# Attention and feed-forward on one core: the first chunks' products are rearranged, the interleaving of first and second products starts one chunk earlier, and loads of q, k, v are tied to attention steps

## The chip, the cores and the metric

The kernel runs on one core of one Trainium2 chip. The metric is the device time of a whole execution in microseconds; smaller is better. One run differs from the next by a few tenths of a per cent. Every run has a state, fast or slow; ratios use fast runs alone. A ratio is the mean time of one kernel's fast runs over the mean of the other's fast runs of the same rounds, so it is not quite the ratio of the medians that are quoted beside it. The span that a profile covers is some 1.8 us shorter than the time.

Engines: PE does the matrix products, DVE and ACT the elementwise work, POOL issues the loads (with the cast from 32-bit to bf16), SP issues stores, small copies and DMA transposes.

## The reference, cut to what matters

```python
# q, k, v: (8 batches, 8 heads, 1024 tokens, 64); E, F: (64, 1024)
k_proj = einsum('ks,bhsd->bhkd', E, k)
v_proj = einsum('ks,bhsd->bhkd', F, v)
attn = softmax(q @ k_proj.T / 8)          # over the 64 projected keys
x = attn @ v_proj                         # -> (8192 tokens, 512)
h = maximum(x @ w_in, 0.0)                # 512 -> 2048
out = (h * h) @ w_out                     # 2048 -> 512
```

## The kernel before: the parts that matter

A batch is cut into two chunks of 512 tokens. Chunk (b, c) needs a first product (x times w_in) and a second one (h squared times w_out). Both exist in two forms: a plain one of 64 matmuls of 512 columns, and a seven-product (Strassen-like) one of 112 matmuls of 256 columns. The second form costs PE less but needs sums of blocks, made on DVE. In most of the kernel, here called the woven part, PE alternates between the first product of one chunk and the second product of the chunk before, in numbered steps of 8 matmuls. A chunk takes 28 steps, and a batch, here called a round, takes 56. Attention of the next batches is slipped in at fixed steps. PE's order is written by hand; the other engines are ordered when the program is built.

The attention code:

```python
soft_pool = ctx.enter_context(tc.tile_pool(name="soft", bufs=3))      # 3 buffers of tag "rs"
# ...
def sums_spread(self, pr):              # sums of the exponentials for two pairs of heads
    ps = att_psum()
    # ... 8 matmuls with ones (32 columns each) ...
    inv = soft_pool.tile([P, 2, TCH], F32, tag="rs", name="inv")
    nc.scalar.activation(inv[:], ps[:], AF.Ln)
    nc.scalar.activation(inv[:], inv[:], AF.Exp, scale=-1.0)
    for j in range(2):
        rs = soft_pool.tile([P, 2, TCH], F32, tag="rs", name="rs")
        for a in range(2):
            have = 32 * (2 * a + j)
            for to in (64 * a, 64 * a + 32):
                nc.sync.dma_start(rs[to:to + 32], inv[have:have + 32])   # 8 small copies on SP
        self.rs[pr + j] = rs

def values(self, pr, spare=False):
    e, rs = self.e.pop(pr), self.rs.pop(pr)
    ps = att_psum()                     # the one attention PSUM buffer of the woven part
    # ... 4 matmuls into ps, then DVE: xT = ps * rs
```

One call takes three buffers of the tag "rs": one inv and two rs. There are three such buffers. In the woven part `att_psum()` has a single buffer: what uses it next must wait until ACT or DVE has read it.

The plan of a round in the woven part (t is the round's first step):

```python
for b in range(1, B - 1):
    t = 56 * (b - 1)
    if b > 1:
        on(t + 1, b + 1, "scores", 3)
    on(t + 3, b + 1, "sums_spread", 2)        # second group of sums of batch b+1
    on(t + 7, b + 1, "values", 0)
    on(t + 10, b + 1, "values", 1)
    on(t + 20, b + 1, "values", 2)
    on(t + 23, b + 1, "values", 3)
    # ...
    if b + 2 < B:
        on(t + 2, b + 2, "transpose_q_dma")   # q of batch b+2, DMA transpose on SP
        if b + 3 < B:
            at(t + 2, begin, b + 3)
            on(t + 3, b + 3, "load_q")
        on(t + 30, b + 2, "project")
        on(t + 32, b + 2, "transpose_k_dma")  # DMA transpose of the projected k, on SP
        if b + 3 < B:
            on(t + 34, b + 3, "load_kv")      # 2 x 1 MB (bf16)
        on(t + 44, b + 2, "scores", 0)
        on(t + 47, b + 2, "scores", 1)
        on(t + 50, b + 2, "sums_spread", 0)   # first group of sums of batch b+2
        on(t + 53, b + 2, "scores", 2)
```

The softmax here doesn't subtract the row's maximum and nothing guards it: scores larger than these inputs give would overflow.

Of the kernel before, what the change touches and what calls it, by code (L numbers as in the profile page):

```python
# [9 lines left out]
P = 128  # L10
F32 = mybir.dt.float32
BF16 = mybir.dt.bfloat16
# [7 lines left out]
def kernel(  # L20
# [11 lines left out]
    nc = tc.nc  # L32
# [31 lines left out]
    part_pool = ctx.enter_context(tc.tile_pool(name="part", bufs=5))  # L64
    out_pool = ctx.enter_context(tc.tile_pool(name="outp", bufs=3))
    psum = ctx.enter_context(tc.tile_pool(name="ps", bufs=1, space=bass.MemoryType.PSUM))
    turn = {"att": 0, "bank": 0, "pairs": 2}

    lent = ctx.enter_context(ExitStack())
    pair_pools = [psum, lent.enter_context(tc.tile_pool(name="ps_lent", bufs=1, space=bass.MemoryType.PSUM))]  # L70
# [7 lines left out]

    def bank(shape=(P, 512), dtype=F32, n=None):
        if n is None:  # L80
            turn["bank"] += 1
            n = turn["bank"]
        return psum.tile(list(shape), dtype, tag=f"bank{n % 4}", name="ps_bank")

# [3 lines left out]
    def load(t, src):  # L88
        return nc.gpsimd.dma_start(t, src)

    def load_batch(name, src, b):
        t = qkv_pool.tile([P, H, NI, D], BF16, name=name)
        load(t[:], tokens(src, b))
        return t


# [30 lines left out]
    for j, (lo, hi) in enumerate(W_IN_PIECES):  # L127
        t = wpool.tile([P, NCB, (hi - lo) * P], BF16, name=f"w_in_{lo}")
        load(t[:], w_in_view[:, :, lo * P:hi * P])
        for fb in range(lo, hi):  # L130
            w_in_at[fb] = (t, fb - lo)
        if j < 2:
            load(V0[:, V_PIECES[j + 1]], tokens(v, 0, h=V_PIECES[j + 1]))
    fn = NFB // WP
    for j in range(WP):
        if j == WP - 1:
            load(Q0[:, :, 4:8, :], tokens(q, 0, i=slice(4, 8)))
        t = wpool.tile([P, fn, DM], BF16, name=f"w_out_{j}")
        load(t[:], w_out_view[:, j * fn:(j + 1) * fn, :])
        w_out_sb.append(t)  # L140
# [31 lines left out]
                    *(w_out_sum[:, n, f] for n in range(4)),  # L172
                )

    def sum_w_in(behind):
        with tc.issue_after(behind.queued.ins):
            for lo, hi in W_IN_PIECES[:3]:
                up, (t, j) = w_in_at[lo][0], w_in_at[HF + lo]
                down = t[:, :, j * P:(j + hi - lo) * P]
                n = NCB // 2  # L180
                left_sums(
                    up[:, 0:n], up[:, n:NCB], down[:, 0:n], down[:, n:NCB],
                    *(w_in_sum[:, m, :, lo:hi].rearrange("p c f k -> p c (f k)") for m in range(4)),
                )
# [37 lines left out]
    class Attention:  # L222
# [10 lines left out]
            self.qT = qt_pool.tile([P, H, NT, P], BF16, name="qT")  # L233
            self.e, self.rs, self.ps_x = {}, {}, {}

        def load_kv(self):
            self.K, self.V = load_batch("K_sb", k, self.b), load_batch("V_sb", v, self.b)

        def load_q(self):
            self.Q = load_batch("Q_sb", q, self.b)  # L240


        def keep_k(self, ps_k, g, second=None):
# [53 lines left out]
            )  # L297


        def transpose_q_chunk(self, c, src, hg):  # L300
            ps = bank([P, 4, 2, P], BF16)
            for hh in range(4):
                for n in range(2):
                    nc.tensor.transpose(
                        ps[:, hh, n, :],
                        src[:, 4 * hg + hh, 4 * c + 2 * n:4 * c + 2 * n + 2, :].rearrange("p i d -> p (i d)"), ident[:]
                    )
            nc.vector.tensor_copy(self.qT[:, 4 * hg:4 * hg + 4, 2 * c:2 * c + 2, :], ps[:])

        def transpose_q(self, pr):  # L310
            ps = bank([P, 2, NT, P], BF16)
# [28 lines left out]

        def exponentials(self, ps):
            e = soft_pool.tile([P, 2, TCH], BF16, name="expT", tag="expT", bufs=4)
            nc.scalar.activation(e[:], ps[:], AF.Exp, scale=SCALE)  # L343
            return e

        def inverse(self, ps):
# [49 lines left out]
        def values(self, pr, spare=False):  # L396

            e, rs = self.e.pop(pr), self.rs.pop(pr)
            if spare:
                ps_x = [bank(), bank()]  # L400
            else:
                ps = att_psum()
                ps_x = [ps[:, par] for par in range(2)]
            for o, par, a, r in VALUE_QUADS:
                nc.tensor.matmul(  # L405
                    ps_x[par][o], lhsT=self.vp[r, 2 * pr + a, :], rhs=e[r, par], start=True, stop=True
                )
            for par in range(2):
                nc.vector.tensor_tensor(  # L409
                    out=self.xT[:, pr, :, par], in0=ps_x[par].rearrange("p (c t) -> p c t", c=2),  # L410
                    in1=rs[:, par].rearrange("p (c t) -> p c t", c=2), op=ALU.mult,
                )
# [25 lines left out]
    class Chunk:  # L438
# [5 lines left out]

        def h_tile(self, kh, part):
            if (kh, part) not in self.h:
                self.h[kh, part] = form_pool.tile([P, 2, HF // 2, HC], BF16, name="h", tag="h", bufs=7)
            return self.h[kh, part]

        def sum_x(self):  # L450
            self.x_sum = x_pool.tile([P, 4, NCB // 2, HC], BF16, name="x_sum")
            n = NCB // 2
            x = [self.xT[:, m:m + n, self.c, a] for m in (0, n) for a in range(2)]
            right_sums(*x, *(self.x_sum[:, m] for m in range(4)))
# [253 lines left out]
    with tc.manual_schedule(engines={PE}):  # L708
# [57 lines left out]
        at(2, att.project_v, V_PIECES[2])  # L766
        at(3, att.chunk_values, 0, 1, (1,))
        at(3, nxt.load_kv)
        at(18, sum_w_in, chunk[0, 0])
        at(21, att.transpose_q_chunk, 1, Q0, 0)  # L770
        at(21, att.transpose_q_chunk, 1, Q0, 1)
        at(21, nxt.load_q)
        at(23, att.chunk_scores, 1, 0)
        at(23, att.chunk_scores, 1, 1)
        at(25, att.sums, 0)
        at(27, att.chunk_values, 1, 0)
        at(27, att.chunk_values, 1, 1)
        at(28, sum_w_out, att)
        at(28, begin, 2)
        at(36, nxt.project)  # L780
        at(36, lambda: atts[2].load_kv())
        at(39, nxt.transpose_q, 0)
        at(39, nxt.transpose_q, 1)
        at(39, nxt.transpose_k)
        at(41, nxt.scores, 0)
        at(41, nxt.scores, 1)
        at(44, nxt.transpose_q, 2)
        at(44, nxt.transpose_q, 3)
        at(44, lambda: atts[2].load_q())
        at(45, nxt.sums, 0)  # L790
        at(47, nxt.scores, 2)
        at(49, nxt.scores, 3)
        at(50, nxt.values, 0)
        at(52, nxt.values, 1)
        at(53, nxt.sums, 2)
        at(59, nxt.values, 2)
        at(60, nxt.values, 3)
        at(60, chunk[1, 1].sum_x)
        at(61, lambda: atts[2].project())
        at(59, begin, 3)  # L800
        at(60, lambda: atts[3].load_kv())
        at(61, lambda: atts[2].transpose_q_dma())
        at(61, lambda: atts[3].load_q())
        run_all(chunk[0, 0].first_cold(), chunk[0, 0].second_cold(), chunk[0, 1].first_plain(), chunk[0, 1].second_seven(*(bank()[:] for _ in range(3))))

        nxt = atts[2]
        at(1, nxt.transpose_k)
        at(3, nxt.scores, 0)
        at(5, nxt.scores, 1)
        at(7, nxt.sums_spread, 0)  # L810
        at(9, nxt.scores, 2)
        at(11, nxt.scores, 3)
        turn["pairs"] = 1
        run_all(chunk[1, 0].first_plain())
        lent.close()
        second_pool = ctx.enter_context(tc.tile_pool(name="ps_second", bufs=1, space=bass.MemoryType.PSUM))

# [7 lines left out]
        def firsts():  # L825
            old = None
            for b in range(1, B):
                for c in range(2):
                    if (b, c) == (1, 0):
                        continue  # L830
                    for g in range(4):
                        new = Group(chunk[b, c], g)
                        for f in F_STEPS:
# [11 lines left out]
        def seconds():  # L845
            for _ in range(LAG):
                yield
            for b in range(1, B):
                for c in range(2):
                    if (b, c) == (B - 1, 1):  # L850
                        return
                    yield from chunk[b, c].second_spread(second_bank)
# [7 lines left out]
        def on(step, b, name, *args):  # L860
            at(step, lambda: getattr(atts[b], name)(*args))

        for b in range(1, B - 1):
            t = 56 * (b - 1)
            if b > 1:
                on(t + 1, b + 1, "scores", 3)
            on(t + 3, b + 1, "sums_spread", 2)
            on(t + 7, b + 1, "values", 0)
            on(t + 10, b + 1, "values", 1)
            on(t + 20, b + 1, "values", 2)  # L870
            on(t + 23, b + 1, "values", 3)
            for c in range(2):
                at(t + 24 + 9 * c, lambda b=b, c=c: chunk[b + 1, c].sum_x())
            if b + 2 < B:
                on(t + 2, b + 2, "transpose_q_dma")
                if b + 3 < B:
                    at(t + 2, begin, b + 3)
                    on(t + 3, b + 3, "load_q")
                on(t + 30, b + 2, "project")
                on(t + 32, b + 2, "transpose_k_dma")  # L880
                if b + 3 < B:
                    on(t + 34, b + 3, "load_kv")
                on(t + 44, b + 2, "scores", 0)
                on(t + 47, b + 2, "scores", 1)
                on(t + 50, b + 2, "sums_spread", 0)
                on(t + 53, b + 2, "scores", 2)
        steps = both()
        run(steps)
        assert not plan, plan
# [31 lines left out]
```

## Time and profile before

The median at the time of the prediction was 482.37 us over 3 runs (480.54 to 484.3).

| what | where it is read | value |
|---|---|---|
| span of the profile | page | 479.9 us |
| PE busy | page | 469.9 us, 98% |
| woven part | windows | 109.1 to 463.8 us, PE idle 1.3 us of 354.7 |
| stage between start and woven part | windows | 25.3 to 109.1 us, PE idle 2.0 us |
| last stretch | windows | 16.1 us |

The first line of the page: busy time of each engine, its share of the span, and the number of instructions.

```profile
PE 469.9 (98%) x4106; PEld 352.0 (73%) x4106; DVE 350.1 (73%) x613; ACT 286.8 (60%) x466; POOL 32.5 (7%) x45
```

The windows, kernel before. Columns: the stretch in us, its length, busy time and instructions of PE, of PE's weight loads, of DVE, ACT and POOL, then the granted clock of PE, the share of the DMA engines, and GB/s.

```profile
25.30:109.10 83.80, 81.82 (x556) 40.43 (x556) 62.89 (x128) 52.27 (x79) 7.39 (x9) 1.00 1.09 194
109.10:463.80 354.70, 353.39 (x3258) 290.26 (x3257) 272.89 (x460) 222.29 (x372) 10.50 (x12) 1.00 0.59 126
463.80:479.90 16.10, 12.36 (x114) 10.83 (x111) 5.59 (x10) 3.46 (x7) 0.00 (x0) 1.00 0.24 82
```

PE is the limit, and in the woven part it hardly ever stands still. PE's list of waits for the same kernel (who waited for whom: us in total, times, longest) names no DMA; its three longest entries are:

```profile
PE ps_second L572 <- ACT ps_second L588: 1.3, 5, 0.3
PE ps_bank L216 <- DVE zeros L118: 1.2, 1, 1.2
PE ps_bank L489 <- DVE xT L434: 1.0, 3, 0.4
```

The timeline of the kernel before, around 139 to 173 us, on four engines (start, duration, engine, line, operation, count): POOL issues K and V, PE does the second group of sums and the first values, ACT does the Ln of both groups, and SP issues eight rs copies, the transpose of q, and eight more rs copies.

```profile
138.99 0.88 POOL L89 DMA_DIRECT2D K_sb<-in_k_dram  x1 [20.60 <-PE ps_att L259]
139.86 0.88 POOL L89 DMA_DIRECT2D V_sb<-in_v_dram  x1
...
166.71 0.41 PE L382 MATMUL ps_att<-expT,ones 64*32 64x512 bf16 x8
170.68 0.41 PE L405 MATMUL ps_att<-expT,vp 64*64 64x512 bf16 x4
...
158.00 1.02 ACT L386 ACTIVATE inv<-ps_att 128x1024 f32<-128x1024 f32 x1 [0.19 <-PE ps_att L382]
169.58 1.02 ACT L386 ACTIVATE inv<-ps_att 128x1024 f32<-128x1024 f32 x1
...
160.48 5.77 SPq L393 DMA_DIRECT2D rs<-inv  x8
167.52 4.58 SPq L321 DMA_TRANSPOSE qT<-Q_sb  x1
172.49 6.17 SPq L393 DMA_DIRECT2D rs<-inv  x8
```

The DMA issues of the same kernel at these times (count, size of one, median us from issue to landing):

```profile
K_sb<-in_k_dram POOLq DMA_DIRECT2D x1, 1024.0 KB, 9.7
V_sb<-in_v_dram POOLq DMA_DIRECT2D x1, 1024.0 KB, 15.2
...
kT<-kp SPq DMA_TRANSPOSE x1, 9.1
...
rs<-inv SPq DMA_DIRECT2D x8, 128.0 KB, 2.7
```

V lands at 139.86 + 15.2, about 155 us. The first rs copy is issued at 160.5 us. The last is issued at 165.5 us and lands 2.5 us later, near 168. The second group's Ln starts at 169.58. In the first round K and V land at 103.7 and 112.2 us, and the copies land in 6.4 us.

### The profile page before, as it was taken

The numbers are of one execution on the slowest core, as the hardware profiler recorded it, in microseconds if no ns is written. First come the engines' busy times: TensorE is split into PE (matmuls) and PEld (weight loads), VectorE is DVE, ScalarE is ACT, GpSimd is POOL, SyncE is SP. The second block draws the span as 40 slices with busy tenths as digits, with TensorE's granted clock in tenths as the row PEclk, the third lists the DMA queues.
The fourth block names the chain that finished last, engine by engine and source line by source line (L and its number), as shares of the span: only waits on it lengthen the run. The fifth ranks groups of instructions, "written<-read, shape, count | busy, mean of one in ns | idle before, by whom it ended". The sixth has DMA issues, their size and how long they took to land.

```text
span 479.9 us, 10022 instructions
## 1 busy us (share of the span) xinstructions
PE 469.9 (98%) x4106; PEld 352.0 (73%) x4106; DVE 350.1 (73%) x613; ACT 286.8 (60%) x466; POOL 32.5 (7%) x45
## 2 busy tenths in 40 slices
PE   8999999999999999999999999999999999999996
PEld 3444445537878788787878778787887778888885
DVE  2456897956996679767897579966797678967671
ACT  2464467397547774578546785477745775565641
POOL 7410010200010000100010000100000000000000
PEclk9999999999999999999999999999999999999999
DMA  9999998999949496767939499495811054101012
GB/s 177 204 206 205 229 165 142 180 225 190 197 83 171 124 200 163 124 130 180 201 105 185 90 221 175 96 160 139 205 54 55 23 133 111 67 23 67 24 66 89
DMA packets 80046, 66.98 MB, mean 140 GB/s; under 512 B 30720, under 2 KB 76032, under 8 KB 80000
## 3 DMA queue, kind: packets, MB, share of 16 engines
q0 software_dynamic: 30640, 29.23, 39.3%
q1 hardware_dynamic: 49216, 36.97, 29.2%
q8 instruction: 32, 0.52, 0.4%
q10 hardware_dynamic: 144, 0.13, 0.1%
q14 instruction: 14, 0.11, 0.1%
HBM read 59.24 MB, written 16.78 MB: 158 GB/s over the span
## 4 chain that ended last, share of the span: by engine, by line
PE 86%; DVE 8%; ACT 4%; issue 1%; DMA 1%; DVEq 0%; ACTq 0%
PE ps_bank L652 34%; PE ps_second L572 33%; PE ps_bank L489 6%; PE ps_att L329 2%; PE ps_att L258 2%; PE ps_second L549 2%; PE ps_att L405 2%; DVE rs L373 1%; DVE w_in_sum L150 1%; DVE w_out_sum L150 1%; DVE xT L434 1%; DVE h L150 1%; PE ps_bank L216 1%; ACT h L485 1%; PE ps_att L382 1%
## 5 line engine op out<-in xcount | busy, mean ns | idle before, releaser
L150 DVE TENSOR_TENSOR h<-h 128x1024 bf16<-128x1024 bf16 (+1 forms) x182 | 108.0, 616 | 39.8 <-ACT h L662 26.0
L652 PE MATMUL ps_bank<-x_sum,w_in_sum 128*128 128x256 bf16 x624 | 93.9, 273 | 0.0
L652 PEld LDWEIGHTS <-w_in_sum 128*128 128x128 bf16 x832 | 78.7, 98 | 16.2 <-issue 7.5
L572 PEld LDWEIGHTS <-h 128*128 128x128 bf16 x832 | 81.3, 98 | 11.8 <-issue 2.2
L544 ACT COPY u<-ps_bank 128x512 f32<-128x512 f32 x107 | 63.2, 591 | 26.0 <-PE ps_bank L652 23.1
L662 ACT ACTIVATE h<-ps_bank 128x512 bf16<-128x512 f32 x104 | 62.9, 605 | 26.3 <-PE ps_bank L652 25.9
L666 DVE CUSTOM_DVE_ANT_0 h<-ps_bank,u 128x512 bf16<-128x512 f32 x104 | 68.9, 685 | 12.5 <-PE ps_bank L652 11.9
L677 ACT COPY ps_bank<-ps_bank 128x512 f32<-128x512 f32 x52 | 29.7, 570 | 68.9 <-PE ps_bank L652 68.9
L652 PEld LDWEIGHTS <-w_in 128*128 128x128 bf16 x624 | 58.8, 98 | 13.9 <-issue 7.2
L572 PEld LDWEIGHTS <-s 128*128 128x128 bf16 x624 | 61.1, 98 | 7.1
L652 PE MATMUL ps_bank<-xT,w_in 128*128 128x256 bf16 x416 | 62.5, 273 | 0.0
L572 PE MATMUL ps_second<-w_out_sum,s 128*128 128x256 bf16 x416 | 62.4, 273 | 0.0
L572 PE MATMUL ps_second<-w_out_sum,h 128*128 128x256 bf16 x416 | 62.2, 273 | 0.0
L572 PE MATMUL ps_second<-w_out,h 128*128 128x256 bf16 x416 | 60.1, 272 | 1.3 <-ACT ps_second L588 1.3
L409 DVE TENSOR_TENSOR xT<-ps_att,rs 128x512 bf16<-128x512 f32 x56 | 36.0, 684 | 15.9 <-PE ps_att L405 15.9
L489 PE MATMUL ps_bank<-xT,w_in 128*128 128x512 bf16 x192 | 45.3, 379 | 1.8 <-DVE xT L434 1.0
L485 ACT ACTIVATE h<-ps_bank 128x512 bf16<-128x512 f32 x48 | 28.1, 605 | 16.1 <-PE ps_bank L489 15.9
L150 DVE TENSOR_TENSOR o_sb<-ps_second,u 128x512 f32<-128x512 f32 x27 | 18.5, 685 | 25.9 <-PE ps_second L572 20.7
L489 PEld LDWEIGHTS <-w_in 128*128 128x128 bf16 x192 | 17.7, 98 | 24.6 <-issue 6.2
L343 ACT ACTIVATE expT<-ps_att 128x1024 bf16<-128x1024 f32 x32 | 32.9, 1036 | 2.9 <-PE ps_att L329 2.5
L652 PE MATMUL ps_bank<-x_sum,w_in 128*128 128x256 bf16 x208 | 31.4, 273 | 0.0
L652 PE MATMUL ps_bank<-xT,w_in_sum 128*128 128x256 bf16 x208 | 31.3, 273 | 0.0
(104 smaller groups left out, 477.7 us busy)
## 6 DMA issues: line engine op xcount, KB each, us to landing
out_dram<-o_sb SPq DMA_DIRECT2D x63, 256.0 KB, 2.4
rs<-inv SPq DMA_DIRECT2D x96, 128.0 KB, 2.9
K_sb<-in_k_dram POOLq DMA_DIRECT2D x7, 1024.0 KB, 9.7
V_sb<-in_v_dram POOLq DMA_DIRECT2D x7, 1024.0 KB, 15.7
Q_sb<-in_q_dram POOLq DMA_DIRECT2D x7, 1024.0 KB, 12.7
w_out<-in_moe_w_out_dram POOLq DMA_DIRECT2D x4, 512.0 KB, 17.5
w_in<-in_moe_w_in_dram POOLq DMA_DIRECT2D x3, 512.0 KB, 14.6
k_f<-in_k_dram SPq DMA_DIRECT2D x1, 512.0 KB, 4.6
```

The lines of the kernel that those rows point to most:

```text
L150: return nc.vector.tensor_tensor(out=o, in0=x, in1=y, op=op)
L258: nc.tensor.matmul(ps[LO, :], lhsT=ET[:, i, :], rhs=self.K[:, :, i, :], start=f, stop=l)
L343: nc.scalar.activation(e[:], ps[:], AF.Exp, scale=SCALE)
L409: nc.vector.tensor_tensor(out=self.xT[:, pr, :, par], in0=ps_x[par].rearrange("p (c t) -> p c t", c=2), in1=rs[:, par].rearrange("p (c t) ...
L485: nc.scalar.activation(h, ps.rearrange("p (a t) -> p a t", a=2), AF.Relu)
L489: nc.tensor.matmul(ps[:], lhsT=w_in_blk(cb, fb), rhs=self.xT[:, cb, self.c].rearrange("p a t -> p (a t)"), start=(cb == 0), stop=(cb == NC ...
L544: nc.scalar.copy(u[:], ps)
L572: nc.tensor.matmul(ps[:, i * HM:(i + 1) * HM], lhsT=self.h_form(n, fb)[:, i * P:(i + 1) * P], rhs=w_out_form(n, fb), start=fresh and i == ...
L652: nc.tensor.matmul(ps[:, j * HC:(j + 1) * HC], lhsT=w_in_form(n, cb, 2 * self.g + j), rhs=self.chunk.x_form(n, cb), start=fresh and j == 0 ...
L662: nc.scalar.activation(self.out(kh, a), ps[:], AF.Relu)
L666: nc.vector._custom_dve(TENSOR_ADD_SAT, out=self.out(kh, a), in0=ps[:], in1=more[:], s0=3.0e38, s1=0.0)
L677: nc.scalar.copy(self.chain[:], self.first[:])
```

## The change

Its intent: fewer PE cycles near the start, as two plain products become seven-product ones, and less interference between the big loads and the small DMAs that attention waits for.

```diff
-    h tiles: bufs=7, x_sum in its own pool (2)
+    h tiles and x_sum share one ring: tag="h", bufs=9
 ...
+    def load_batch(name, src, b, behind=None):
+        dma = load(t[:], tokens(src, b))
+        if behind:
+            tc.add_manual_dep(dma.ins, behind().ins.name, ..., reason="load behind")
 ...
-  run_all(chunk[0, 0].first_cold(), chunk[0, 0].second_cold(),
-          chunk[0, 1].first_plain(), chunk[0, 1].second_seven(...))
-  ... run_all(chunk[1, 0].first_plain())
+  run_all(chunk[0, 0].first_cold(), chunk[0, 1].first_plain(sums=False))
+  ... run_all(chunk[0, 0].second_seven(*banks))
   # attention of batch 0's second half and of batch 1 now by chunks; batch 1's q in two half loads
 ...
   firsts():   from chunk (1, 0) on, was (1, 1)
   seconds():  from chunk (0, 1) on, was (1, 0)
 ...
-  for b in range(1, B - 1):      t = 56 * (b - 1)
+  for b in range(B - 1):         t = 56 * (b - 1) + 28
-  on(t + 3,  b + 3, "load_q")
+  on(t + 11 if b else 5, b + 3, "load_q", (lambda b=b: atts[b + 1].done) if b else None)
-  on(t + 30, b + 2, "project")
-  on(t + 32, b + 2, "transpose_k_dma")
-  on(t + 34, b + 3, "load_kv")
+  on(t + (32 if b else 35), b + 2, "project")
+  on(t + (34 if b else 36), b + 2, "transpose_k_dma")
+  on(t + (45 if b else 46), b + 3, "load_kv", lambda b=b: atts[b + 2].done)
```

The diff is cut and joined: the lines on the tiles, on the two start points and on the loop are told in short form. `done` is the last exponential or the last multiply of values that this batch has run. So K and V now wait for the exponential of the first scores, and Q waits for the second values.

More of the change, by code (lines that the diff above doesn't have):

```diff
@@ L66 @@
     psum = ctx.enter_context(tc.tile_pool(name="ps", bufs=1, space=bass.MemoryType.PSUM))
-    turn = {"att": 0, "bank": 0, "pairs": 2}
+    turn = {"att": 0, "bank": 0, "step": 1, "pairs": 2}
     lent = ctx.enter_context(ExitStack())
@@ L80, in bank @@
         if n is None:
-            turn["bank"] += 1
+            turn["bank"] += turn["step"]
             n = turn["bank"]
@@ L89, in load @@
         return nc.gpsimd.dma_start(t, src)
-    def load_batch(name, src, b):
+    def load_batch(name, src, b, behind=None):
         t = qkv_pool.tile([P, H, NI, D], BF16, name=name)
-        load(t[:], tokens(src, b))
+        dma = load(t[:], tokens(src, b))
+        if behind:
+            tc.add_manual_dep(
+                dma.ins, behind().ins.name,
+                mybir.DependencyInfo(mybir.DependencyClass.Sync, mybir.DependencyReason.DATA), reason="load behind",
+            )
         return t
@@ L133 @@
             load(V0[:, V_PIECES[j + 1]], tokens(v, 0, h=V_PIECES[j + 1]))
+        if j == 2:
+            for g in range(2):
+                load(Q0[:, half[g], 4:8, :], tokens(q, 0, h=half[g], i=slice(4, 8)))
     fn = NFB // WP
     for j in range(WP):
-        if j == WP - 1:
-            load(Q0[:, :, 4:8, :], tokens(q, 0, i=slice(4, 8)))
         t = wpool.tile([P, fn, DM], BF16, name=f"w_out_{j}")
@@ L173, in sum_w_out, with sum_w_in @@
                 )
-    def sum_w_in(behind):
+    def sum_w_in(behind, piece):
         with tc.issue_after(behind.queued.ins):
-            for lo, hi in W_IN_PIECES[:3]:
+            for lo, hi in W_IN_PIECES[piece:piece + 1]:
                 up, (t, j) = w_in_at[lo][0], w_in_at[HF + lo]
@@ L234, in __init__, with load_kv, load_q, load_q_halves @@
             self.e, self.rs, self.ps_x = {}, {}, {}
-        def load_kv(self):
-            self.K, self.V = load_batch("K_sb", k, self.b), load_batch("V_sb", v, self.b)
-        def load_q(self):
-            self.Q = load_batch("Q_sb", q, self.b)
+        def load_kv(self, behind=None):
+            self.K, self.V = (load_batch(n, src, self.b, behind) for n, src in (("K_sb", k), ("V_sb", v)))
+        def load_q(self, behind=None):
+            self.Q = load_batch("Q_sb", q, self.b, behind)
+        def load_q_halves(self):
+            self.Q = qkv_pool.tile([P, H, NI, D], BF16, name="Q_sb")
+            for i in (slice(0, 4), slice(4, 8)):
+                load(self.Q[:, :, i, :], tokens(q, self.b, i=i))
         def keep_k(self, ps_k, g, second=None):
@@ L297, in transpose_k_dma, with transpose_q_chunk @@
             )
-        def transpose_q_chunk(self, c, src, hg):
+        def transpose_q_chunk(self, c, src, hg, copy=nc.vector.tensor_copy):
             ps = bank([P, 4, 2, P], BF16)
+            src = self.Q if src is None else src
             for hh in range(4):
@@ L307, in transpose_q_chunk @@
                     )
-            nc.vector.tensor_copy(self.qT[:, 4 * hg:4 * hg + 4, 2 * c:2 * c + 2, :], ps[:])
+            copy(self.qT[:, 4 * hg:4 * hg + 4, 2 * c:2 * c + 2, :], ps[:])
         def transpose_q(self, pr):
@@ L342, in exponentials @@
             e = soft_pool.tile([P, 2, TCH], BF16, name="expT", tag="expT", bufs=4)
-            nc.scalar.activation(e[:], ps[:], AF.Exp, scale=SCALE)
+            self.done = nc.scalar.activation(e[:], ps[:], AF.Exp, scale=SCALE)
             return e
@@ L408, in values @@
             for par in range(2):
-                nc.vector.tensor_tensor(
+                self.done = nc.vector.tensor_tensor(
                     out=self.xT[:, pr, :, par], in0=ps_x[par].rearrange("p (c t) -> p c t", c=2),
@@ L446, in h_tile @@
             if (kh, part) not in self.h:
-                self.h[kh, part] = form_pool.tile([P, 2, HF // 2, HC], BF16, name="h", tag="h", bufs=7)
+                self.h[kh, part] = form_pool.tile([P, 2, HF // 2, HC], BF16, name="h", tag="h", bufs=9)
             return self.h[kh, part]
         def sum_x(self):
-            self.x_sum = x_pool.tile([P, 4, NCB // 2, HC], BF16, name="x_sum")
+            self.x_sum = form_pool.tile([P, 4, NCB // 2, HC], BF16, name="x_sum", tag="h", bufs=9)
             n = NCB // 2
@@ L768 @@
         at(3, nxt.load_kv)
-        at(18, sum_w_in, chunk[0, 0])
-        at(21, att.transpose_q_chunk, 1, Q0, 0)
-        at(21, att.transpose_q_chunk, 1, Q0, 1)
-        at(21, nxt.load_q)
-        at(23, att.chunk_scores, 1, 0)
-        at(23, att.chunk_scores, 1, 1)
-        at(25, att.sums, 0)
-        at(27, att.chunk_values, 1, 0)
-        at(27, att.chunk_values, 1, 1)
-        at(28, sum_w_out, att)
-        at(28, begin, 2)
-        at(36, nxt.project)
-        at(36, lambda: atts[2].load_kv())
@@ L782 @@
-        at(39, nxt.transpose_q, 0)
-        at(39, nxt.transpose_q, 1)
-        at(39, nxt.transpose_k)
-        at(41, nxt.scores, 0)
-        at(41, nxt.scores, 1)
-        at(44, nxt.transpose_q, 2)
-        at(44, nxt.transpose_q, 3)
-        at(44, lambda: atts[2].load_q())
-        at(45, nxt.sums, 0)
-        at(47, nxt.scores, 2)
-        at(49, nxt.scores, 3)
-        at(50, nxt.values, 0)
-        at(52, nxt.values, 1)
-        at(53, nxt.sums, 2)
-        at(59, nxt.values, 2)
-        at(60, nxt.values, 3)
@@ L798 @@
-        at(60, chunk[1, 1].sum_x)
-        at(61, lambda: atts[2].project())
-        at(59, begin, 3)
-        at(60, lambda: atts[3].load_kv())
-        at(61, lambda: atts[2].transpose_q_dma())
-        at(61, lambda: atts[3].load_q())
-        run_all(chunk[0, 0].first_cold(), chunk[0, 0].second_cold(), chunk[0, 1].first_plain(), chunk[0, 1].second_seven(*(bank()[:] for _ in range(3))))
-        nxt = atts[2]
-        at(1, nxt.transpose_k)
-        at(3, nxt.scores, 0)
-        at(5, nxt.scores, 1)
@@ L810 @@
-        at(7, nxt.sums_spread, 0)
-        at(9, nxt.scores, 2)
-        at(11, nxt.scores, 3)
-        turn["pairs"] = 1
-        run_all(chunk[1, 0].first_plain())
+        at(6, att.transpose_q_chunk, 1, Q0, 0)
+        at(7, att.transpose_q_chunk, 1, Q0, 1)
+        at(7, nxt.load_q_halves)
+        at(7, att.chunk_scores, 1, 0)
+        at(8, att.chunk_scores, 1, 1)
+        at(9, att.chunk_sums, 1, 0)
+        at(10, att.chunk_sums, 1, 1)
+        at(12, att.chunk_values, 1, 0)
+        at(14, att.chunk_values, 1, 1)
@@ new lines @@
+        for n, step in enumerate((9, 17, 18)):
+            at(step, sum_w_in, chunk[0, int(n > 0)], n)
+        at(18, chunk[0, 0].sum_h, 0)
+        at(20, chunk[0, 0].sum_h, 1)
+        at(22, sum_w_out, chunk[0, 1])
+        at(31, nxt.transpose_q_chunk, 0, None, 0, nc.scalar.copy)
+        at(24, begin, 2)
+        run_all(chunk[0, 0].first_cold(), chunk[0, 1].first_plain(sums=False))
+        base = turn["bank"]
+        banks = [bank(n=base + n)[:] for n in (1, 4, 3)]
+        turn["bank"], turn["step"], turn["att"] = base + 2, 0, 0
@@ new lines @@
+        at(1, nxt.transpose_q_chunk, 0, None, 1, nc.scalar.copy)
+        at(2, nxt.project)
+        at(2, lambda: atts[2].load_kv())
+        at(5, nxt.transpose_k)
+        at(7, nxt.chunk_scores, 0, 0)
+        at(8, nxt.chunk_scores, 0, 1)
+        at(8, nxt.transpose_q_chunk, 1, None, 0)
+        at(9, nxt.chunk_sums, 0, 0)
+        at(10, nxt.chunk_sums, 0, 1)
+        at(10, nxt.transpose_q_chunk, 1, None, 1)
+        at(10, lambda: atts[2].load_q())
+        at(11, nxt.chunk_values, 0, 0)
@@ L815 @@
+        at(12, nxt.chunk_values, 0, 1)
+        at(12, chunk[1, 0].sum_x)
+        at(12, chunk[0, 1].sum_h, 0)
+        at(12, nxt.chunk_scores, 1, 0)
+        at(14, nxt.chunk_sums, 1, 0)
+        at(14, chunk[0, 1].sum_h, 1)
+        run_all(chunk[0, 0].second_seven(*banks))
+        turn["pairs"], turn["bank"] = 1, base
         lent.close()
@@ L828, in firsts @@
                 for c in range(2):
-                    if (b, c) == (1, 0):
-                        continue
                     for g in range(4):
@@ L847, in seconds @@
                 yield
-            for b in range(1, B):
+            for b in range(B):
                 for c in range(2):
+                    if (b, c) == (0, 0):
+                        continue
                     if (b, c) == (B - 1, 1):
@@ L861, in on @@
             at(step, lambda: getattr(atts[b], name)(*args))
-        for b in range(1, B - 1):
-            t = 56 * (b - 1)
-            if b > 1:
-                on(t + 1, b + 1, "scores", 3)
-            on(t + 3, b + 1, "sums_spread", 2)
-            on(t + 7, b + 1, "values", 0)
-            on(t + 10, b + 1, "values", 1)
-            on(t + 20, b + 1, "values", 2)
-            on(t + 23, b + 1, "values", 3)
-            for c in range(2):
-                at(t + 24 + 9 * c, lambda b=b, c=c: chunk[b + 1, c].sum_x())
+        on(1, 1, "chunk_scores", 1, 1)
@@ new lines @@
+        on(5, 1, "chunk_values", 1, 0)
+        on(11, 1, "chunk_sums", 1, 1)
+        on(14, 1, "chunk_values", 1, 1)
+        for b in range(B - 1):
+            t = 56 * (b - 1) + 28
+            if b:
+                on(t + 1, b + 1, "scores", 3)
+                on(t + 3, b + 1, "sums_spread", 2)
+                on(t + 7, b + 1, "values", 0)
+                on(t + 10, b + 1, "values", 1)
+                on(t + 20, b + 1, "values", 2)
+                on(t + 23, b + 1, "values", 3)
+                at(t + 24, lambda b=b: chunk[b + 1, 0].sum_x())
+            at(t + 51, lambda b=b: chunk[b + 1, 1].sum_x())
@@ L874 @@
             if b + 2 < B:
-                on(t + 2, b + 2, "transpose_q_dma")
+                on(t + 2 if b else 4, b + 2, "transpose_q_dma")
                 if b + 3 < B:
-                    at(t + 2, begin, b + 3)
-                    on(t + 3, b + 3, "load_q")
-                on(t + 30, b + 2, "project")
-                on(t + 32, b + 2, "transpose_k_dma")
-                if b + 3 < B:
-                    on(t + 34, b + 3, "load_kv")
-                on(t + 44, b + 2, "scores", 0)
-                on(t + 47, b + 2, "scores", 1)
@@ L885 @@
-                on(t + 50, b + 2, "sums_spread", 0)
-                on(t + 53, b + 2, "scores", 2)
+                    at(t + 2 if b else 4, begin, b + 3)
+                    on(t + 11 if b else 5, b + 3, "load_q", (lambda b=b: atts[b + 1].done) if b else None)
+                on(t + (32 if b else 35), b + 2, "project")
+                on(t + (34 if b else 36), b + 2, "transpose_k_dma")
+                on(t + (44 if b else 45), b + 2, "scores", 0)
+                if b + 3 < B:
+                    on(t + (45 if b else 46), b + 3, "load_kv", lambda b=b: atts[b + 2].done)
@@ L887 @@
+                on(t + (47 if b else 48), b + 2, "scores", 1)
+                on(t + (50 if b else 51), b + 2, "sums_spread", 0)
+                on(t + (53 if b else 54), b + 2, "scores", 2)
         steps = both()
```

## The prediction

> **What bounds the kernel now.** The PE, in program order. The page gives PE 98% busy at clock 1.0; the Trainium skill ("Perfetto Trace Analysis", Identifying the Most-Contended Engine) says that matmul busy time is no measure of headroom, so I count work in the timeline. A 128x512 matmul is spaced 0.2155 us (20 in 4.31 us; the skill's "TensorE: Matmul & The Clock Gate", Back-to-back issue gap, has 216 ns: this trace agrees). Four 256-column matmuls take 0.437 us. From 109.1 to 463.8 us, the woven part, PE idles only 1.3 us (windows), all on one ACT copy (line 588). From 25.3 to 109.1 it idles 2.0 us, some 1.4 of it short waits in the stage that the change rewrites. The start (before 25 us) and the last 16 us stay.
>
> **PE work.** Plain products cost 64 x 0.2155 = 13.8 us, seven-product ones 28 x 0.437 = 12.2 us.
> - The second product of the first chunk and the first product of chunk (1,0) become seven-product ones: -3.1 us.
> - Attention of batch 0's second half and of batch 1 goes by chunks: three more groups of sums of 0.34 us: +1.0. Batch 2's kT by DMA: -0.3.
> - Some five more insertions of attention between products, 0.09 us each: +0.45.
> - The short waits of the old stage go: -1.4.
>
> **New waits.**
> - Q of batch 1. Loading in the first 54 us is limited by transfers: 1 MB (bf16) takes about 5 us; K and V of batch 1 land at 47 and 54 us, Q at 60 (issues, time to landing). Without the four early stores V should land near 52, the first half of Q near 54.5. PE reaches its transposes at about 53.5: 25.4 + 11.4 + 3.7 of attention + 12.9 of first products. Wait about 1 us, perhaps 3.
> - The handover to the woven part. Within about 13 us ACT gets four exponentials (1.03), six Ln/Exp (1.02 to 1.06) and copies (0.59), about 13 us in sum, and the woven part's second banks reuse the lent pair that the last sums sit in. About 1.5 us.
> - DVE loses the 32-row copies of sums (12 x 0.69 us) but gets sums of h and x early: about 0.5 us for PE.
>
> **Deferred loads** (Q behind values, K and V behind scores) should move nothing by themselves: in the woven part PE never waits for a DMA. They shorten kT's transpose to landing (9.0 us now, with K and V loading beside it), which the closer scores need. The shared ring of nine h/x_sum buffers equals the old 7 + 2 and should not bind.
>
> Sum: -3.1 + 1.0 - 0.3 + 0.45 - 1.4 + 3.0 = about -0.4 us, the waits being my least certain term; half as long, it is -2. I take -2: **480.4 us**, range 477.0 to 484.2. Chances: faster by over 2% 0.03, within 2% 0.94, slower 0.03.
>
> **What would show it.** The line-495 group (64 plain second products) is gone; line-489 products fall from 192 to 128 and 256-column first products rise by 112. PE's wait list shows the transposes of Q waiting for a DMA near 53 us, and second-product or bank waits for ACT near 73 us. The woven part starts about 33 us earlier and lasts 28 steps (some 30 us) more, with PE idle under 3 us. kT lands in 2 to 4 us in the later batches.
>
> **What would make it wrong.** Q or V landing far later (several us of PE wait), a backlog at the handover carried through the first woven steps, a ring wait repeated in each chunk (14 times), or none of these waits, when it would come out near 478.

## The result, and the profile after

The changed kernel takes 497.59 us (median of 4 runs, 495.98 to 498.23) against 482.13 us (4 runs). The ratio is 1.0312, with a 95% interval of 1.0265 to 1.036: it is slower by 3%.

Busy time by engine, kernel after, from its page:

```profile
PE 471.1 (95%) x4224; PEld 364.0 (73%) x4230; DVE 350.9 (71%) x612; ACT 294.6 (59%) x476; POOL 34.0 (7%) x47
```

The windows of the kernel after, cut at its own borders of the stages:

```profile
24.20:77.60 53.40, 50.52 (x386) 27.36 (x388) 43.01 (x91) 35.67 (x53) 6.73 (x8) 0.97 1.06 171
77.60:479.90 402.30, 387.93 (x3553) 315.67 (x3550) 293.79 (x495) 246.65 (x409) 13.14 (x15) 0.99 0.62 129
479.90:496.00 16.10, 12.39 (x114) 10.86 (x111) 5.62 (x10) 3.49 (x7) 0.00 (x0) 1.00 0.24 83
```

The woven part starts 31.5 us earlier (77.6 for 109.1), lasts 47.6 us longer (402.3 for 354.7), and the last stretch is the same. That is the 16.1 us between the spans. PE's idle time in the woven part went from 1.3 to 14.4 us. PE's list of waits, kernel after:

```profile
PE ps_att L417 <- ACT inv L398: 14.0, 5, 3.6
PE ps_bank L316 <- DMA Q_sb<-in_q_dram: 2.1, 1, 2.1
PE ps_bank L501 <- DVE xT L446: 1.5, 6, 0.3
```

Line 417 is the values matmul and line 398 is the Ln of sums. The wait comes once in each of five rounds. The same place in a round as shown above, timeline of the kernel after:

```profile
158.69 0.88 POOL L89 DMA_DIRECT2D K_sb<-in_k_dram  x1 [31.87 <-ACT expT L355]
159.56 0.88 POOL L89 DMA_DIRECT2D V_sb<-in_v_dram  x1
...
172.24 0.41 PE L394 MATMUL ps_att<-expT,ones 64*32 64x512 bf16 x8
178.80 0.64 PE L417 MATMUL ps_att<-expT,vp 64*64 64x512 bf16 x4 [2.52 <-ACT inv L398]
...
177.73 1.02 ACT L398 ACTIVATE inv<-ps_att 128x1024 f32<-128x1024 f32 x1 [2.53 <-DMA out_dram<-o_sb]
...
166.01 4.99 SPq L405 DMA_DIRECT2D rs<-inv  x8
173.97 7.45 SPq L333 DMA_TRANSPOSE qT<-Q_sb  x1
181.51 7.28 SPq L405 DMA_DIRECT2D rs<-inv  x8
```

The DMA issues of the kernel after at these times:

```profile
K_sb<-in_k_dram POOLq DMA_DIRECT2D x1, 1024.0 KB, 9.1
V_sb<-in_v_dram POOLq DMA_DIRECT2D x1, 1024.0 KB, 19.2
...
kT<-kp SPq DMA_TRANSPOSE x1, 2.3
...
rs<-inv SPq DMA_DIRECT2D x8, 128.0 KB, 7.2
```

K and V are now issued 7.3 us ahead of the first rs copy, in place of 21.5 us, and V lands near 179 us. The copies run beside them and land in 7.2 us in place of 2.7. kT's transpose, which the deferral protects, is faster: 2.3 us for 9.1. But the last rs copy now lands at 177.5 us. Only then may Ln write inv's buffer, and only when Ln has read the sums may PE write values into the one attention PSUM buffer. In the first of these waits the chain of waits names the copies (start, duration, what):

```profile
109.58 7.37 DMA rs<-inv
...
117.02 1.03 ACT inv L398
...
118.10 0.64 PE ps_att L417 x4
```

In three of the five rounds the profile puts Ln's wait down to a store that landed at about the same time, as in the timeline above. Ln neither reads nor writes anything that a store touches, so that name is a guess by time. In all five rounds the last rs copy lands 0.07 to 0.26 us before Ln begins; experiment e8 tests the link.

There is a second cost. The windows of the kernel after, around the first and the second wait:

```profile
114.50:118.10 3.60, 0.01 (x3) 0.04 (x2) 0.11 (x1) 1.05 (x2) 0.00 (x0) 0.86 1.49 273
118.10:123.90 5.80, 5.80 (x28) 3.60 (x27) 1.29 (x2) 3.37 (x5) 0.00 (x0) 0.50 1.11 180
...
178.80:184.00 5.20, 5.20 (x35) 3.45 (x35) 1.48 (x3) 3.19 (x5) 0.00 (x0) 0.70 1.04 229
```

After the wait of 3.6 us PE ran at half clock for 5.8 us, and after the one of 2.5 us at 0.70 for 5.2 us. That loses 5.8 x 0.50 + 5.2 x 0.30, about 4.5 us. The three later waits, of 2.5 to 2.7 us, were not followed by a drop. The Trainium skill ("TensorE: Matmul & The Clock Gate", What's actually happening) describes a free-running activity window of about 3.4 us, and has PE throttled to half its clock after an idle window. This trace agrees in part: the wait of 3.6 us was followed by a clock of 0.50. But a wait of 2.5 us, shorter than that window, was followed by a drop too, and the three others of about that length were not. No run here shows what decides between them.

### The profile page after: what moved, and what is told of

It reads as the page before. It is cut to its first block, busy times and chain, and to the rows that moved or that the text cites. A ratio compares the mean times of both kernels' runs of the same rounds, so it can differ in the third digit from the quotient of the medians.

```text
span 496.0 us, 10295 instructions
## 1 busy us (share of the span) xinstructions
PE 471.1 (95%) x4224; PEld 364.0 (73%) x4230; DVE 350.9 (71%) x612; ACT 294.6 (59%) x476; POOL 34.0 (7%) x47
## 4 chain that ended last, share of the span: by engine, by line
PE 76%; DMA 13%; ACT 4%; DVE 3%; SPq 2%; issue 1%; ACTq 0%; DVEq 0%
PE ps_bank L664 31%; PE ps_second L584 30%; DMA Q_sb<-in_q_dram 5%; DMA rs<-inv 4%; PE ps_bank L561 3%; PE ps_att L269 3%; DMA out_dram<-o_sb 2%; SPq L405 2%; PE ps_att L417 2%; PE ps_second L561 2%; PE ps_bank L501 2%; PE ps_att L341 2%; ACT inv L398 1%; DVE xT L446 1%; DMA k_f<-in_k_dram 1%
## 5 line engine op out<-in xcount | busy, mean ns | idle before, releaser
L156 DVE TENSOR_TENSOR h<-h 128x1024 bf16<-128x1024 bf16 (+1 forms) x176 | 106.9, 637 | 37.8 <-ACT h L674 33.9
L664 PE MATMUL ps_bank<-x_sum,w_in_sum 128*128 128x256 bf16 x672 | 102.1, 275 | 0.0
L664 PEld LDWEIGHTS <-w_in_sum 128*128 128x128 bf16 x896 | 84.9, 98 | 18.5 <-issue 8.8
L584 PEld LDWEIGHTS <-h 128*128 128x128 bf16 x896 | 88.3, 99 | 11.6 <-issue 0.4
L678 DVE CUSTOM_DVE_ANT_0 h<-ps_bank,u 128x512 bf16<-128x512 f32 x112 | 73.8, 685 | 15.3 <-PE ps_bank L664 14.4
L664 PEld LDWEIGHTS <-w_in 128*128 128x128 bf16 x672 | 63.6, 99 | 16.2 <-issue 8.9
L664 PE MATMUL ps_bank<-xT,w_in 128*128 128x256 bf16 x448 | 68.3, 276 | 0.0
L584 PE MATMUL ps_second<-w_out_sum,s 128*128 128x256 bf16 x448 | 67.7, 274 | 0.0
L584 PE MATMUL ps_second<-w_out,h 128*128 128x256 bf16 x448 | 66.1, 276 | 0.2 <-ACT ps_second L600 0.2
L421 DVE TENSOR_TENSOR xT<-ps_att,rs 128x512 bf16<-128x512 f32 x48 | 30.9, 685 | 32.2 <-PE ps_att L417 32.2
L584 PE MATMUL ps_second<-w_out,s 128*128 128x256 bf16 x224 | 33.6, 273 | 0.0
L501 PE MATMUL ps_bank<-xT,w_in 128*128 128x512 bf16 x124 | 30.9, 387 | 1.9 <-DVE xT L446 1.5
```

What stands on the lines that cost most here:

```text
L156: return nc.vector.tensor_tensor(out=o, in0=x, in1=y, op=op)
L421: self.done = nc.vector.tensor_tensor(out=self.xT[:, pr, :, par], in0=ps_x[par].rearrange("p (c t) -> p c t", c=2), in1=rs[:, par].rearran ...
L501: nc.tensor.matmul(ps[:], lhsT=w_in_blk(cb, fb), rhs=self.xT[:, cb, self.c].rearrange("p a t -> p (a t)"), start=(cb == 0), stop=(cb == NC ...
L584: nc.tensor.matmul(ps[:, i * HM:(i + 1) * HM], lhsT=self.h_form(n, fb)[:, i * P:(i + 1) * P], rhs=w_out_form(n, fb), start=fresh and i == ...
L664: nc.tensor.matmul(ps[:, j * HC:(j + 1) * HC], lhsT=w_in_form(n, cb, 2 * self.g + j), rhs=self.chunk.x_form(n, cb), start=fresh and j == 0 ...
L678: nc.vector._custom_dve(TENSOR_ADD_SAT, out=self.out(kh, a), in0=ps[:], in1=more[:], s0=3.0e38, s1=0.0)
```

## The experiments

My theory after the result: the deferred K and V loads meet the first group's rs copies; late copies hold inv's buffer; Ln waits; PE's values matmuls wait for Ln. Rivals: the new weaving or the shared ring of nine buffers makes the waits; or the deferred Q load does. Ten kernels ran and all gave the right result. The times of the kernel before in the same rounds had medians of 481.1 to 482.0 us.

| run | median us | ratio to before, 95% interval | PE waits that matter (profile, us) |
|---|---|---|---|
| after | 497.59 | 1.0312 (1.0265 to 1.036) | Ln 14.0, Q 2.1 |
| e1 | 482.86 | 1.0039 (1.0014 to 1.0064) | Ln 3.1, Q 0.8 |
| e2 | 496.74 | 1.0312 (1.0263 to 1.0361) | Ln 13.7, Q 0.9 |
| e3 | 494.91 | 1.0278 (1.0248 to 1.0308) | Ln 9.4 |
| e4 | 482.51 | 1.0002 (0.9958 to 1.0047) | V 2.8, Q 1.5 |
| e5 | 534.99 | 1.1082 (1.1048 to 1.1115) | DVE 42.1, Ln 2.6, Q 2.0 |
| e6 | 534.16 | 1.1103 (1.1067 to 1.114) | DVE 39.6, Ln 4.6 |
| e7 | 498.27 | 1.0344 (1.0314 to 1.0375) | Ln 13.4 |
| e8 | 492.91 | 1.0219 (1.0193 to 1.0246) | ACT 5.6, DVE 5.0, Q 2.3 |
| e9 | 477.05 | 0.9904 (0.9885 to 0.9923) | V 0.5 |
| e10 | 480.47 | 0.9972 (0.9937 to 1.0006) | Q 0.3 |

In e4 one run of four, and in e5 two of six, were slow ones; the medians include them, the ratios don't. e5's profile fell in a slow run, so e6's trace, which is of a fast run, is used for both.

### e1: K and V early again

```diff
-  on(t + (45 if b else 46), b + 3, "load_kv", lambda b=b: atts[b + 2].done)
+  on(t + (34 if b else 37), b + 3, "load_kv")
```

> The changed kernel with one line altered: K and V of the batch after next are loaded at step 34 again and wait for no attention step; Q stays deferred, all else as changed. Theory (the deferred K and V loads run beside the first round's rs copies, those land 7.3 us after issue in place of 2.4, the inv buffer stays taken, Ln of the second round waits, and the PE's values matmuls wait for that Ln): rs copies land in 2.4 to 3 us, the values matmuls wait 0 to 1 us in all in place of 14.0, the clock drops of the woven part go, and the time is 480 to 483 us. Rival 1 (the new weaving of seconds or the shared ring of nine buffers causes the waits): waits and time stay, 496 to 499. Rival 2 (the deferred Q load causes them): the same, 496 to 499. A cost may appear: kT's transposes land in 9 us again and scores may wait a little.

One line takes back nearly all of the loss: 482.86 us. The rs copies land in a median of 3.0 us over the whole run (5.7 in the kernel after), and four of the five Ln waits are gone. The one left, 3.1 us, is in the first round, whose loads come at their own step: there V lands at 117.2 us, so it still runs beside the copies. The theory gained and both rivals lost, though the wait left is above the 0 to 1 us that I wrote. kT's transposes land in 8.9 us again, and scores waited for kT once, 0.3 us.

### e2: Q early again, K and V still deferred

```diff
-  on(t + 11 if b else 5, b + 3, "load_q", (lambda b=b: atts[b + 1].done) if b else None)
+  on(t + 3 if b else 5, b + 3, "load_q")
```

> The changed kernel with only the Q load put back: at step 3 of each round and behind nothing; K and V stay deferred. Theory: K and V loads still meet the rs copies, so five waits of the values matmuls stay, 13 to 16 us in sum, and the time is 496 to 501 us. Rival 2 (Q's deferral is at fault): the waits go and the time is 480 to 484.

Nothing changed: 496.74 us, and 13.7 us of waits for Ln in five rounds. Q's deferral neither costs nor gains here.

### e3: the kernel before, with K and V deferred

```diff
-  on(t + 34, b + 3, "load_kv")
+  on(t + 45, b + 3, "load_kv", lambda b=b: atts[b + 2].done)
```

> The kernel before with only K and V deferred as in the change (step 45, behind the exponential of the first scores); four such loads. Theory: the wait of the values matmuls for Ln appears in the old kernel too, four times 2.5 to 3.6 us, rs copies beside loads land in about 7 us, and with a clock drop or two the time is 492 to 498 us against 482. Rival 1 (it takes the new weaving): no waits, 480 to 484.

The old kernel with this one part of the change becomes almost as slow as the changed one: 494.91 us. The wait appears in each of the four rounds that have such a load:

```profile
PE ps_att L410 <- ACT inv L391: 9.4, 4, 2.5
```

Its total, four times about 2.35 us, is a little under the 2.5 to 3.6 each that I wrote; the rs copies of one such round landed in 7.0 us. With e1 this settles it from both sides: the deferral of K and V alone brings most of the loss (2.8% of 3.1%), and without it most of the loss is gone, whatever the weaving.

### e4: K and V later still

```diff
-  if b + 3 < B:
-      on(t + (45 if b else 46), b + 3, "load_kv", lambda b=b: atts[b + 2].done)
+  if b:
+      on(t + 10, b + 2, "load_kv", lambda b=b: atts[b + 1].done)   # next round's step 10
```

> The changed kernel with K and V loaded later still: at step 10 of the next round, behind the last values product of that round's first half, ahead of Q, so that neither kT's transpose nor any rs copy meets them. Theory: rs copies land in 2.4 to 3 us, kT in 2.3, no values wait; the projection 22 steps later finds K and V landed (15 us of transfers in about 20 us). Time 478 to 481 us, a little under e1. If deferral of K and V as such is at fault (rival), it stays at 496 or more, or the projection waits for V by some us per round.

All waits for Ln are gone and kT's transposes land in a median of 3.4 us, so a later load as such is harmless if it misses the first group's copies. Loads do still run beside the second group's, against what I wrote: some of these took up to 9.6 us, and no wait for Ln came of it. The time, 482.51 us with a ratio of 1.0002, is above what I wrote (481.4 is the mean of the three fast runs): the projection waited twice for V (2.8 us) and the transposes for batch 1's Q (1.5 us).

### e5 and e6: K and V between the two groups of sums

e5 puts the load of e4 at step 2 of the round in place of step 10. e6 does the same and issues batch 1's first half of Q ahead of its V:

```diff
+      on(t + 2, b + 2, "load_kv", lambda b=b: atts[b + 1].done)
 # e6 too, at the start:
+      K of batch 1; then q[:, :, 0:4]; then V; then q[:, :, 4:8]     # was K, V, q halves
```

> The changed kernel with K and V loaded at step 2 of the next round, behind the exponential of that round's fourth scores: after the first round's rs copies have landed, before values, and about 8 us sooner than in e4, where V came 2.8 us too late for two projections. Theory: first-round rs copies land in 2.4 to 3 us, second-round ones later (5 to 7 us) but these are not needed for 12 us; no wait of values for Ln, no wait of the projection for V; what is left is the wait for batch 1's Q, 1 to 2 us. Time 477 to 480 us. If rs copies of the second round matter as much as those of the first, waits of values return and the time is over 485.

> As e5, and batch 1's first half of Q is issued ahead of its V. Theory: that half lands some 5 us sooner, at about 50 us, so the transposes at 53.5 us wait for nothing; V lands at about 55, before the projection at 58. Saves the 0.8 to 2.1 us wait and, in runs where the clock drops after it, up to 2 us more: 475 to 479 us, the best kernel of the study. If V becomes the late one, the projection waits for it by 1 to 3 us and it equals e5.

Both were badly wrong: 535 and 534 us. In the round shown below the first group's copies did land in about 2.5 us, as expected, and e6's wait for Q did go. In the first round Ln still waited (4.6 us in e6). But PE now waited for DVE, as e6's list of waits says:

```profile
PE ps_att L422 <- DVE xT L426: 27.0, 4, 7.6
PE ps_bank L669 <- DVE h L683: 12.6, 4, 4.3
```

PE's mean clock in the woven part also fell, to 0.94. The timeline of e6 on POOL and SP shows where the waits come from:

```profile
177.41 0.87 POOL L89 DMA_DIRECT2D K_sb<-in_k_dram  x1 [45.01 <-ACT expT L360]
178.27 0.88 POOL L89 DMA_DIRECT2D V_sb<-in_v_dram  x1
...
171.34 6.23 SPq L410 DMA_DIRECT2D rs<-inv  x8
178.86 19.43 SPq L338 DMA_TRANSPOSE qT<-Q_sb  x1
198.40 4.96 SPq L410 DMA_DIRECT2D rs<-inv  x8
```

The issue of qT's transpose holds SP for 19.43 us in place of 4.58, with the loads started just before it, and the second group's rs copies stand behind it in SP's order. Once issued, they land in 2.8 us. I had looked at the landing of DMAs and not at how long their issue takes. e10 tests this.

### e7 and e8: is inv's buffer the link?

A fourth rs buffer does not fit, so the control e7 shrinks two pools and e8 adds the buffer:

```diff
 # e7 and e8
-  part bufs=5, outp bufs=3
+  part bufs=4, outp bufs=2
 # e8 only
-  soft bufs=3
+  soft bufs=4
```

> Control for e8: the changed kernel with two output buffers in place of three and four part buffers in place of five, which frees room for one more rs buffer. Theory: the waits of values stay (13 to 15 us) and the time is 496 to 501 us, the smaller pools costing 0 to 3 us.

> As e7 with four rs/inv buffers in place of three, loads as in the change. Theory (the link between slow rs copies and the PE is the inv buffer: with three buffers and three allocations per round, each inv takes the buffer of the inv before): Ln of the second round no longer waits for the copies, so PE's wait for Ln falls from 14 us to under 4, though the copies still take about 7 us; the multiply on DVE then waits for rs, 2 to 4 us each round. Time 8 to 14 us under e7. Rival (the PE would have waited for the late rs data itself, whatever the buffers): PE waits stay above 10 us, now for DVE, and the time is within 3 us of e7.

e7 is as slow as the kernel after (498.27 us, Ln waits 13.4 us). In e8 the waits of values for Ln are gone altogether, with the loads where the change put them and the rs copies still at a median of 6.0 us. So inv's buffer is the link from the copies to Ln, and not the stores that the profile named. The gain, 5.4 us between the medians, is less than the 8 to 14 that I wrote, and only a third of what e7 loses to the kernel before. PE now waits 5.6 us for ACT and 5.0 us for DVE:

```profile
PE ps_second L584 <- ACT ps_second L600: 5.6, 7, 1.2
PE ps_bank L664 <- DVE h L678: 5.0, 4, 1.6
```

The rival is half right: a part of the cost of late copies stays when Ln is freed. That these waits come from the late rs data was not tested by itself, so the path of the other two thirds in e8 stays open. The last link, from Ln to PE by the one attention PSUM buffer, is read from the code and the list of waits; no run changes it.

### e10: the rs copies ahead of qT's transpose

```diff
 # e5, and
-  on(t + 2 if b else 4, b + 2, "transpose_q_dma")
+  at(t + 8, q_dma_after_spread, b)     # issued on SP after the last rs copy of sums_spread(2)
```

> e5 (K and V at step 2, 535 us) with one more move: the issue of qT's transpose on SP comes after the second round's rs copies in place of before them. Theory for e5's 53 us: with K and V running, the issue of qT's transpose holds SP for 17.8 us in place of 4.6, and the rs copies queue behind it in SP's order, so values multiply late on DVE. Then here the rs copies leave SP some 12 us sooner and the 30 us of PE waits for DVE xT and the 12 us for DVE h fall under 8 us in sum: 482 to 495 us, the stores behind the transpose perhaps costing some. Rival (K and V slow the rs copies' own transfers, order on SP matters little): stays over 520 us.

From 534.99 to 480.47 us by putting one issue behind others on SP (the call `begin` of batch b + 3 moved along with it, from step 2 to 8; the diff is cut). No wait for DVE xT or DVE h in the woven part is left in PE's list. The transpose's issue still took 9.9 to 11.5 us in the rounds with loads; now nothing urgent stands behind it. The second group's copies, now beside the loads, land in about 7 us, and that costs PE nothing that its list shows. So e5's loss was the order on SP.

### e9: the best version

e4, with batch 1's Q order of e6, and the projection two steps later:

```diff
-  on(t + (32 if b else 35), b + 2, "project")
-  on(t + (34 if b else 36), b + 2, "transpose_k_dma")
+  on(t + (34 if b else 35), b + 2, "project")
+  on(t + 36, b + 2, "transpose_k_dma")
```

> e4 (K and V at step 10 of the next round) with two more moves: batch 1's first half of Q issued ahead of its V, which in e6 took away the transposes' wait for Q, and the projection two steps later (34 for 32; kT's transpose 36 for 34), as V came up to 1.7 us late in e4 and kT lands in about 3 us with 8 steps left. Theory: no PE wait for a DMA is left, PE idle about 4 us less than e4's 13.1, clock near 1.0: 475 to 478 us, 1 per cent faster than the kernel before. If scores wait for kT, or V of batch 1 is late, 478 to 481.

It takes 477.05 us, a ratio of 0.9904 (0.9885 to 0.9923): 1% faster than the kernel before, by six fast runs. That is within the 2% that the verdict calls the same, but clear of the noise. Its windows:

```profile
24.00:75.25 51.25, 50.19 (x397) 27.22 (x396) 43.86 (x93) 35.47 (x53) 6.88 (x8) 1.00 1.12 179
75.25:460.11 384.86, 383.98 (x3552) 313.71 (x3549) 293.98 (x495) 246.14 (x409) 13.16 (x15) 1.00 0.64 135
460.11:476.20 16.09, 12.39 (x114) 10.86 (x111) 5.62 (x10) 3.50 (x7) 0.00 (x0) 1.00 0.24 83
```

The woven part starts 33.9 us earlier than in the kernel before and lasts 30.2 us longer (384.86 less 354.70); the last stretch is the same. That is 3.7 us of gain, about what the rearranged products were meant to bring. Against the changed kernel three moves were made at once, so e9 does not say what each is worth.

## Why the prediction was wrong, point by point

- **Total.** I predicted 480.4 us and gave 3% to "slower by over 2%". It came out at 497.59. The sum of PE work was about right; one term that I had set to zero was some 18 us.
- **The step that failed**, as the prediction put it: "Deferred loads (Q behind values, K and V behind scores) should move nothing by themselves: in the woven part PE never waits for a DMA." The second half was a true reading of the list of waits, but it does not support the first half. That list shows waits under the old order, not the margin. In the later rounds K and V had landed 5 us before the rs copies began, and inv's buffer came free about 1.5 us before Ln took it, 0.35 us in the first round; both could be read from the timeline of the kernel before. Deferral by 11 steps moved 2 MB of loads onto the copies. The copies went from 2.7 to 7.2 us, PE waited 14.0 us in five rounds, and about 4.5 us went in clock drops after two of these waits. e1 and e3 show that it is this part of the change, e2 that it is not Q's, and e8 that inv's buffer passes the delay on to Ln.
- **PE work.** Predicted: the work terms -3.1 + 1.0 - 0.3 + 0.45 and -1.4 for old short waits, together -3.35 us. In e9, where nearly no wait is left, the span is 3.7 us shorter than before: the sum agrees, though its terms were not measured one by one. The counts came out too: the plain second products are gone, and 256-column first products went from 1456 to 1568, which is 112 more.
- **Start of the woven part.** Predicted about 33 us earlier: 31.5 in the kernel after, 33.9 in e9. Predicted some 30 us longer: 47.6 in the kernel after and 30.2 in e9. PE's idle time in it was to stay under 3 us and was 14.4.
- **Wait for batch 1's Q.** Predicted about 1 us, perhaps 3, near 53 us: it was 2.07 us and ended at 55.2. I had not counted the slower clock after it (0.56 of full speed for 3.8 us, some 1.7 us).
- **The handover** (1.5 us on ACT) and **DVE's early sums** (0.5 us): neither appeared. PE waited 0.2 us for line 600 on ACT at that place. The second-bank wait of the old kernel (1.3 us), on whose fate the prediction says nothing, also went to 0.2.
- **kT.** Predicted to land in 2 to 4 us: 2.3. The deferral does what it was made for; it is only that nothing waited for kT before.
- **The shared ring** was not to bind: right, no wait of that kind shows, and e9 is fast with it.
- **What would make it wrong**: my list had late Q or V, a backlog at the handover, and a ring wait repeated in each chunk. The true cause was a wait repeated in each round, but on another ring, that of rs and inv.

## What to carry to other kernels

A list of waits without DMAs does not say that loads may be moved freely. Before moving a load, write down when it will run, which small transfers run then, and how long a delay of those can be borne; buffers that are reused in strict turn carry a delay to engines which never touch the data. The issue of a DMA can hold its queue far longer beside large loads (here 19.43 us in place of 4.58), so put what is urgent ahead of it. And a wait on PE can cost clock as well: in the kernel after, waits of 2.1, 2.5 and 3.6 us were followed by losses of about 1.7, 1.6 and 2.9 us, and three others by none.

## What the Trainium skill lacked or had wrong

- "DMA: Bandwidth & Descriptors", Issuing engines are not separate DMA queues. It says that DMAs from all issuers run on the same 16 engines and interleave. The runs agree: rs copies issued on SP went from 2.7 to 7.2 us when POOL's loads ran. It has no figure for what a small transfer then takes; here eight copies of 128 KB beside two loads of 1 MB land 7.0 to 7.6 us after issue (medians of a group), in place of 2.3 to 2.8.
- The same section calls the sequencer's time to start a DMA "usually small relative to the DMA itself". For the DMA transpose of 1 MB it was not: 4.58 us of about 6.5 with no load beside it, and 19.43 us of 21.6 in e6 beside the loads. Moving the next copies ahead of that issue was worth 54 us (534.99 to 480.47, e5 and e10).
- "DMA: Bandwidth & Descriptors", DMA Transpose (X-bar): it has no time for which such an issue holds its engine while other transfers run. Here it was 4.58 us alone, 9.9 to 11.5 us in e10 and 16.2 to 19.6 us in e6, and the copies behind it on SP waited that long.
- "TensorE: Matmul & The Clock Gate", What's actually happening. It has the throttle after an idle window of about 3.4 us. Here idle times of 2.1 and 2.5 us, shorter than that window, were also followed by clocks of 0.56 and 0.70, while three of 2.5 to 2.7 us were not.
- No page gives a way to read the margin of a wait that does not show yet; here it was 0.35 to 2.2 us on inv's buffer.
